# Row sums ahead of a subtraction, a copy moved to ScalarE, and three steps re-placed in a linear-attention and gated-MLP kernel

## The chip, the cores and the metric

The kernel runs on one core of a Trainium2 chip. The metric is the device time of one execution in microseconds (us). The core has five engines that run their own instruction lists in order and meet through semaphores: TensorE (PE in the profile; its weight loads are shown apart as PEld), VectorE (DVE), ScalarE (ACT), GpSimd (POOL) and SyncE (SP), which mostly issues DMAs.

## The reference

Two parts in a row. The first is an attention without a score matrix, for 8 batches, 8 heads, 576 rows and a head size of 64; the second an MLP with a gate on the 4608 rows of 512 that come out of it.

```python
q_s = exp(q - max(q, -1)); q_s = q_s / (sum(q_s, -1) + 1e-09)     # softmax along the head size
k_s = exp(k - max(k, 2));  k_s = k_s / (sum(k_s, 2) + 1e-09)      # softmax along the rows
kv  = einsum('bhsd,bhse->bhde', k_s, v)
x   = einsum('bhsd,bhde->bhse', q_s, kv)                          # then to [4608, 512]
h = x @ w_in                                                      # 512 -> 2048
g = h * (1.0 / (1.0 + exp(-beta * h)))
out = g @ w_out                                                   # 2048 -> 512
```

## The kernel before

**Slabs.** The rows are cut into nine slabs of 512. Slabs 0 to 7 hold the first 512 rows of each batch, slab 8 the 64 rows that each batch has left over. The main loop runs over `t`, the slab whose MLP is computed; the attention of a later batch (t + 1, and its preparation from t + 2 on) is woven into it.

**Pass 1** of a slab computes `h` transposed, 16 tiles of four matmuls of 128x512 (`pass1_tile`, with the first three tiles interleaved in `pass1_lead`). ScalarE evacuates each tile with Silu into GT (L746), VectorE scales it by 1/beta (`scale_g`, L769) and, after tiles 8, 12, 14 and 16, forms sums of halves of GT, GS1 and GS2 (L800, L805).

**Pass 2** of slab 0 is a plain product with WOUT (`pass2_group`). In the other slabs, `pass2_fast` forms the 2x2 block product with seven block products in place of eight, each of 16 matmuls of 128x256, in three PSUM banks: `s`, `z5` and `z2`. The order on TensorE is s and z5 interleaved, z2, then onto the same banks a second z5 product ("product 1" below), a second z2 product ("2"), a third z5 product ("3") and a third z2 product ("4"). Between them stand evacuations: TS gets a copy of s (L915), less z5 (L918), less z2 (L924); then ScalarE copies z5 and z2 to the output tile O2S (`copy`, L882), and VectorE adds TS to the last ones (`last`, L894). Since the later products add onto the same bank, product 1 may start only when L918 has read z5, product 2 when L924 has read z2, product 3 when the copy of z5 is done, and product 4 when the copy of z2 is done. `g_diff(0)` and `g_diff(1)` (L812, VectorE) turn halves of GT into differences that products 3 and 4 read.

**Attention of a batch.** ScalarE takes exps of q (EQ), k (EK) and the left-over k rows (EKR). `norm_main` has two parts: row sums and their reciprocals on VectorE (`sums`, L357 and L359, into QS and QI) and the multiplication EQ by QI (`mult`, L361, on GpSimd in the later slabs). `turn` has SP issue a DMA transpose of EQ into QT. `norm_turn` does all of this for two of four head pairs. `cast_v` (L377) and `cast_vr` (L391) cast v and its left-over rows to bf16 (VB, VR). `kv_steps` forms kv on TensorE (L482, for batches 0 and 1 L406), followed by VectorE's reciprocal RC (L490) and the scaled KVD (L449 or L459). `quad` and `out_step` multiply QT by KVD (L554, L406) into XT, the input of pass 1 of the next slab.

**Order of the work.** Each operation is recorded in the program's order with what it reads and writes; `Program.plan` derives from that the semaphore waits, and each engine gets its operations in the order recorded. Two devices place the side work. `todo` is a list of pairs (tick, function): each matmul of pass 1 is a tick (64 in all), each of pass 2 is 32/56 of one, and a function is recorded as soon as its tick is reached. `hooks` are lists of functions that `pass2_fast` records at its points `at(0)` (before s), `at(1)` (after the copy to TS), `at(2)` (after L918), `at(3)` (after L924), `at(4)` and `at(5)` (after ScalarE's copies of z5 and z2), `at(6)` and `at(7)` (after the two last additions). So in slabs 1 and 2 the eight exps stand on ScalarE behind the last Silu, the row sums on VectorE behind the subtractions L918 and L924, and `silu_table` loads ScalarE's table for the next pass 1 at `at(4)`.

**The end.** Each store has its own semaphore. Behind its last DMA, SP waits for all of them one after another (L149 to L151), in the order of their names.

Of the kernel before, what the change touches and what calls it, by code (L numbers as in the profile page):

```python
# [20 lines left out]
NG = NF // 2  # L21
# [8 lines left out]
PE, ACTE, DVE, POOL, SP = "tensor", "scalar", "vector", "gpsimd", "sync"  # L30
# [14 lines left out]
class Program:  # L45
# [12 lines left out]
    def add(self, eng, fn, r=(), w=(), bank=(), slot=None, after=(), war=False):  # L58
        op = Op(eng, fn, slot)
        op.pos = len(self.ops)  # L60
        deps = op.deps
        deps.extend(after)
        for k in r:
            deps.extend(self.writer.get(k, ()))
            self.readers.setdefault(k, []).append(op)
        for k in w:
            for d in self.readers.get(k, ()):
                if d is not op and (war or not self._same(d, op)):
                    deps.append(d)
            for d in self.writer.get(k, ()):  # L70
                if not self._same(d, op):
                    deps.append(d)
            self.readers[k] = []
            self.writer[k] = [op]
        for k in bank:
            t = self.touch.setdefault(k, {})
            for e, d in t.items():
                if e != eng:
                    deps.append(d)
            t[eng] = op  # L80
        if eng == POOL and slot is None:
            if self.pool is not None:
                deps.append(self.pool)
            self.pool = op
        self.ops.append(op)
        return op
# [42 lines left out]
    def emit(self, nc, es):  # L129
        counts, waits = self.plan()  # L130
        sems = {}
        for key in counts:
            sems[key] = es.enter_context(nc.semaphore("s_" + "_".join(str(x) for x in key)))
        by = {e: [] for e in (PE, ACTE, DVE, POOL, SP)}
        for op, w in zip(self.ops, waits):
            by[op.eng].append((op, w))

        def run(eng):
            def body(h):
                for op, w in by[eng]:  # L140
                    for key, n in w:
                        h.wait_ge(sems[key], n)
                    ins = op.fn(h)
                    if op.slot is not None:
                        ins.then_inc(sems[op.count[0]], 16)
                    elif op.inc:
                        ins.then_inc(sems[op.count[0]], 1)
                if eng == SP:
                    for key, n in sorted(counts.items(), key=str):  # L149
                        if key[0] == "dma" and str(key[1]).startswith("out"):  # L150
                            h.wait_ge(sems[key], n)  # L151
            return body

        with nc.Block() as blk:
            for e in (PE, ACTE, DVE, POOL, SP):
                getattr(blk, e)(run(e))


def bass_efficient_attn_shen__then__act_swish_beta_kernel(
# [12 lines left out]
    with ExitStack() as es:  # L172
        def sb(name, shape, dt):
# [33 lines left out]
        TS = sb("TS", [128, 512], F32)  # L207
# [12 lines left out]
        PS = [es.enter_context(nc.psum_tensor(f"PS{i}", [128, 512], F32)) for i in range(8)]  # L220
# [4 lines left out]
        P = Program()  # L225
        add = P.add
# [6 lines left out]
            r=["ts"], w=["idb"])  # L233
# [152 lines left out]
        def cast_vr(b, hs=(0, 1), after=()):  # L386
            pi = (b // 2) % 2
            for h in hs:
                o = bass.AP(VR[pi][h], 64 * h * NHP * VW, [[NHP * VW, 64], [HW, H], [1, D]])
                a = bass.AP(VRF, 64 * h * 512, [[512, 64], [D, H], [1, D]])  # L390
                add(POOL, lambda e, o=o, a=a: e.tensor_copy(o, a),  # L391
                    r=[("vrf", h), ("vrone", pi, h), ("vr0", pi, h)], w=[("vr", pi, h)],
                    after=after)
# [208 lines left out]
        def turn(b, hp0, n):  # L602
            i = b % 2
            o = bass.AP(QT[i], hp0 * 512, [[2048, 128], [128, 4 * n], [1, 128]])
            a = bass.AP(EQ[i], hp0 * 512, [[2048, 128], [1, 512 * n]])
            add(SP, lambda e: e.dma_start_transpose(o, a),
                r=[("eq", i, hp) for hp in range(hp0, hp0 + n)],
                w=[("qt", i, hp) for hp in range(hp0, hp0 + n)], slot=f"tq{i}{hp0}")
# [26 lines left out]

        def attn_late(b):
            if b < 4:
                x = 100 if b == 2 else 97
                return [(x, steps(kv_all, b)), (x + .1, lambda: g_diff(1)),
                        (118, one(quad, b, (0,)))]  # L640
            return [(96, steps(kv_all, b)), (99, lambda: g_diff(1)), (112, one(quad, b))]
# [193 lines left out]
        def pass2_fast(t, tick, hooks):  # L835
# [71 lines left out]
            def prod_s(part):  # L907
# [4 lines left out]
            prod(z5, *gs2(0), *wo(1, 1), True, False, range(0, 6))  # L912
            prod_s(range(6, NG))
            prod(z5, *gs2(0), *wo(1, 1), True, False, range(6, NG))
            add(DVE, lambda e: e.tensor_copy(TS[:, :], PS[s][:, :]), r=[("ps", s)], w=["ts"],  # L915
                bank=[s])
            at(1)
            add(DVE, lambda e: e.tensor_tensor(TS[:, :], TS[:, :], PS[z5][:, :], ALU.subtract),  # L918
                r=["ts", ("ps", z5)], w=["ts"], bank=[z5])
# [35 lines left out]
        for t in range(NSLAB):  # L955
            todo = []
            if t == 0:
                todo = [(x, steps(t_steps, 1, (hp,), NOW, ACTE))
                        for hp, x in enumerate((97, 106, 114, 119))]
                todo += [(107, one(exp_kr_s, 1))]  # L960
                todo += [(x, one(exp_k, 1, hp, 1)) for hp, x in enumerate((108, 115, 120, 125.5))]
                todo += [(x, one(cast_v, 1, hp, DVE))
                         for hp, x in ((1, 118.5), (2, 123), (3, 127))]
                todo += [(x, steps(kv_steps, 1, (hp,), NOW))
                         for hp, x in enumerate((118, 122, 126))]
                todo += [(x, steps(out_step, 1, hp, NOW, ACTE)) for hp, x in enumerate((122.5, 125))]
                todo += [(117, one(o2_evac, 0, 0, 3, ACTE))]
                todo += [(2, steps(out_step, 0, 3, HEAD, DVE))]
            elif t < 4:
                todo = attn_late(t + 1)  # L970
                if t > 1:
                    todo += [(1.5, one(quad, t, (1,)))]
                if t == 3:
                    todo += [(4, one(norm_turn, 4, 2))]
                if t == 1:
                    todo += [(1, steps(out_step, 1, 2, (3,), ACTE)),
                             (3, steps(kv_steps, 1, (3,), (7,))),
                             (6, steps(out_step, 1, 3, (7,), DVE)),
                             (6.1, one(w_sum, 2, 4, 4)), (6.2, one(w_diff, 0)),
                             (6.3, one(w_diff, 1))]  # L980
            elif t < 7:
                todo = attn(t + 1)
            elif t == 7:
                todo = spread(outr_steps(1), 32, 48)
# [59 lines left out]
            def on(n, fn, *a):  # L1044
                hooks.setdefault(n, []).append(lambda: fn(*a))
# [8 lines left out]
                add(ACTE, lambda e: e.activation(DUMMY[:, 2:3], WARM[:, 0:1], ACT.Silu),  # L1054
                    r=["warm"], w=["dummy"])

            def casts(b):
                g = P.writer[("gs2", NG - 1)]
                if b % 2 == 0:
                    cast_vr(b, after=g)  # L1060
                for hp in range(NHP):
                    cast_v(b, hp, after=g)

            if t == 1:
                on(0, exps, 2)
                on(0, casts, 2)
                on(2, norm_turn, 2, 0)
                on(3, norm_turn, 2, 2)
                on(3, g_diff, 0)
                on(4, silu_table)  # L1070
                on(3, load, 4)
            elif t == 2:
                on(0, exps, 3)
                on(2, norm_turn, 3, 0)
                on(3, norm_turn, 3, 2)
                on(3, g_diff, 0)
                on(3, load, 5)
                on(4, exp_q, 4)
                on(4, silu_table)
                on(4, casts, 4)  # L1080
                on(6, norm_turn, 4, 0)
            elif t == 3:
                on(0, exp_k, 4)
                on(0, exp_kr, 4)
                on(0, exp_q, 5)
                on(3, g_diff, 0)
                on(4, norm_turn, 5, 0)
                on(5, norm_turn, 5, 2)
                on(4, exp_qr, 1)
                on(5, exp_k, 5)  # L1090
                on(5, norm_turn_rem)
                on(5, casts, 5)
                on(5, load, 6)
                on(7, load_rem, "qrf", qt_h, QRF, 4)
            elif t + 2 < B:
                b = t + 2
                on(0, exps, b)
                on(0, casts, b)
                if t == 4:
                    on(0, load, 7)  # L1100
                on(3, norm_turn, b, 0)
                on(4, norm_turn, b, 2)
# [40 lines left out]
```

The softmax here doesn't subtract the row's maximum and nothing guards it: scores larger than these inputs give would overflow.

## Time and profile before

| | us |
|---|---|
| median of 5 runs | 273.04 |
| lowest, highest | 272.77, 274.46 |
| the profiled execution | 272.99 |
| its span, first to last instruction | 271.2 |
| TensorE's mean granted clock, share of full | 0.998 |
| slab 1, pass 1, from its first matmul | 45.7 to about 61 |
| slab 1, pass 2 | 60.9 to 75 |
| slab 2, pass 2 | 89.2 to 104 |
| last addition on VectorE (L894) | 267.61 to 268.03 |

A line of a timeline gives start, duration, engine, line, operation, output<-input with its shape, and in brackets how long the engine was idle before it and what released it. Rows that follow each other closely on an engine are merged (x2, x4). PEld rows show when TensorE was ready for a product: a wait of TensorE shows there first. "issue" as a releaser means that the profile shows nothing that was waited for.

### The profile page before, as it was taken

How to read it: one execution, taken by the hardware profiler on the slowest of the kernel's cores; microseconds unless marked ns; L12 is line 12 of the kernel's file. 1: busy time of each engine (PE TensorE's matmuls, PEld its weight loads, DVE VectorE, ACT ScalarE, POOL GpSimd, SP SyncE). 2: the span in 40 equal slices, each digit the busy share in tenths (PEclk: the TensorE clock that was granted, in tenths of full speed). 3: DMA queues.
4: the chain of work that ended last, by engine and by line, in shares of the span. 5: the costliest groups of instructions: out<-in, count | busy, mean ns of one | idle time of the engine just before them, and what ended most of it. 6: DMA issues, size and time to landing. Idle time of an engine off the chain costs nothing.

```text
span 271.2 us, 4991 instructions
## 1 busy us (share of the span) xinstructions
PE 263.0 (97%) x1974; PEld 163.5 (60%) x1993; DVE 193.2 (71%) x407; ACT 181.5 (67%) x289; POOL 63.5 (23%) x80
## 2 busy tenths in 40 slices
PE   8999999999999999999999999999999999999994
PEld 2544444348744875468645864587458745874683
DVE  4964586887957798868778876887588448626762
ACT  4898658799467974887778937892883387018610
POOL 2790000006630089100810680036000100000000
PEclk9999999999999999999999999999999999999999
DMA  7999999989699129940499899603600130012006
GB/s 219 318 204 206 228 324 350 297 232 372 161 324 324 51 47 290 288 155 2 77 268 273 245 360 178 195 3 78 213 2 0 36 140 2 0 64 93 0 1 156
DMA packets 59367, 45.95 MB, mean 169 GB/s; under 512 B 28608, under 2 KB 58320, under 8 KB 58320
## 3 DMA queue, kind: packets, MB, share of 16 engines
q1 hardware_dynamic: 54480, 40.90, 53.6%
q0 software_dynamic: 4240, 4.19, 9.4%
q10 hardware_dynamic: 624, 0.53, 0.6%
q8 instruction: 16, 0.26, 0.4%
q14 instruction: 7, 0.06, 0.1%
HBM read 36.71 MB, written 9.44 MB: 170 GB/s over the span
## 4 chain that ended last, share of the span: by engine, by line
PE 77%; DMA 9%; DVE 4%; POOL 4%; ACT 2%; issue 1%; SPq 0%; POOLq 0%
PE PS L406 43%; PE PS L846 31%; DMA WOUT<-in_moe_w_out_dram 5%; DMA QF<-in_q_dram 3%; POOL WIN L670 2%; PE PS L482 1%; PE PS L554 1%; DMA QT<-EQ 1%; DVE EQ L361 1%; DVE QS L357 1%; POOL EQ L361 1%; ACT EQ L319 1%; POOL VB L377 1%; ACT L1054 0%; POOL VR L391 0%
## 5 line engine op out<-in xcount | busy, mean ns | idle before, releaser
L406 PE MATMUL PS<-XT,WIN 128*128 128x512 bf16 x560 | 125.2, 379 | 1.2 <-issue 0.3
L746 ACT ACTIVATE GT<-PS,BETA 128x512 bf16<-128x512 f32 x144 | 95.2, 690 | 39.5 <-PE PS L406 39.2
L406 PEld LDWEIGHTS PS<-XT,WIN 128*128 128x128 bf16 x576 | 55.0, 98 | 64.8 <-DVE XT L596 0.7
L769 DVE TENSOR_SCALAR GT<-GT,RB 128x512 bf16<-128x512 bf16 x144 | 52.7, 387 | 38.4 <-ACT GT L746 37.6
L361 POOL TENSOR_TENSOR EQ<-EQ,QI 128x1024 bf16<-128x1024 bf16 (+1 forms) x13 | 25.6, 1968 | 47.2 <-DVE QI L359 46.5
L846 PE MATMUL PS<-WOUT,GS 128*128 128x256 bf16 x256 | 31.1, 273 | 0.0
L846 PE MATMUL PS<-WSUM,GT 128*128 128x256 bf16 x256 | 30.1, 273 | 1.0 <-ACT O2S L882 1.0
L846 PE MATMUL PS<-WOUT,GT 128*128 128x256 bf16 x256 | 29.8, 273 | 0.0
L846 PEld LDWEIGHTS PS<-WSUM,GT 128*128 128x128 bf16 x256 | 24.8, 98 | 5.0 <-ACT O2S L882 1.2
L882 ACT COPY O2S<-PS 128x512 f32<-128x512 f32 (+1 forms) x17 | 9.4, 560 | 26.1 <-PE PS L846 26.1
L846 PEld LDWEIGHTS PS<-WOUT,GT 128*128 128x128 bf16 x256 | 24.8, 98 | 2.9
L846 PEld LDWEIGHTS PS<-WOUT,GS 128*128 128x128 bf16 x256 | 24.8, 98 | 3.0
L319 ACT ACTIVATE EQ<-QF 128x512 bf16<-128x512 f32 x32 | 17.9, 620 | 7.3 <-DMA QF<-in_q_dram 7.3
L805 DVE TENSOR_TENSOR GS<-GT 128x512 bf16<-128x512 bf16 (+2 forms) x32 | 21.9, 685 | 0.0
L812 DVE TENSOR_TENSOR GT<-GT 128x2048 bf16<-128x2048 bf16 x16 | 21.7, 1381 | 0.0
L377 POOL CAST VB<-VF 128x512 bf16<-128x512 f32 x24 | 16.5, 688 | 22.0 <-DVE GS L805 13.3
L357 DVE TENSOR_REDUCE QS<-EQ 128x16 f32<-128x1024 bf16 (+1 forms) x20 | 19.7, 984 | 1.0 <-ACT EQ L319 1.0
L319 ACT ACTIVATE EK<-KF 128x512 bf16<-128x512 f32 x32 | 18.1, 620 | 0.0
L894 DVE TENSOR_TENSOR O2S<-TS,PS 128x512 f32<-128x512 f32 (+1 forms) x17 | 10.8, 647 | 9.6 <-PE PS L846 9.6
L846 PE MATMUL PS<-WSUM,GS 128*128 128x256 bf16 x128 | 16.6, 273 | 0.0
L406 PE MATMUL PS<-WOUT,GT 128*128 128x512 bf16 x62 | 15.0, 379 | 0.1
L846 PEld LDWEIGHTS PS<-WSUM,GS 128*128 128x128 bf16 x128 | 12.5, 98 | 3.2
(90 smaller groups left out, 208.9 us busy)
## 6 DMA issues: line engine op xcount, KB each, us to landing
out_dram<-O2S SPq DMA_DIRECT2D x8, 1024.0 KB, 4.9
QF<-in_q_dram SPq DMA_DIRECT2D x6, 1024.0 KB, 6.3
KF<-in_k_dram SPq DMA_DIRECT2D x6, 1024.0 KB, 9.5
VF<-in_v_dram SPq DMA_DIRECT2D x6, 1024.0 KB, 12.6
KF<-in_k_dram SPq DMA_DIRECT2D x8, 256.0 KB, 5.5
VF<-in_v_dram SPq DMA_DIRECT2D x8, 256.0 KB, 5.5
WOUT<-in_moe_w_out_dram POOLq DMA_DIRECT2D x4, 512.0 KB, 16.2
WIN<-in_moe_w_in_dram POOLq DMA_DIRECT2D x3, 512.0 KB, 9.0
```

The lines of the kernel that those rows point to most:

```text
L319: add(ACTE, lambda e, o=o, a=a: e.activation(o, a, ACT.Exp), r=[(name + "f", i, hp)], w=[("e" + name, i, hp)])
L357: add(DVE, lambda e: e.tensor_reduce(s_, a, AX.X, ALU.add), r=ks, w=[("qs", i, hp0)])
L361: add(eng, lambda e: e.tensor_tensor(a, a, vb, ALU.mult), r=ks + [("qi", i, hp0)], w=ks)
L377: add(eng, lambda e: (e.copy if eng == ACTE else e.tensor_copy)(o, a), r=[("vf", i, hp), ("vone", i)], w=[("vb", i, hp)], after=after)
L406: add(PE, lambda e: e.matmul(o, l, r_, start=start, stop=stop), r=r, w=w, bank=[bk])
L746: add(ACTE, lambda e: e.activation(GT[:, f, :], PS[bk][:, :], ACT.Silu, scale=BETA[:, f:f + 1]), r=[("ps", bk), "beta"], w=[("gt", f, 0), ...
L769: add(DVE, lambda e: e.tensor_scalar(GT[:, f, :], GT[:, f, :], RB[:, f:f + 1], None, ALU.mult), r=k + ["rb"], w=k)
L805: add(DVE, lambda e: e.tensor_tensor(GS2[:, i:i + n, :], GT[:, i:i + n, :], GT[:, i + NG:i + NG + n, :], ALU.add), r=[k_ for f in (i, i + ...
L812: add(DVE, lambda e: e.tensor_tensor(gv(f, th, NG), gv(f, th, NG), gv(f, 1 - th, NG), ALU.subtract), r=gk(f, 0, NG) + gk(f, 1, NG), w=gk(f ...
L846: add(PE, lambda e, l=l, r_=r_, st=st, u=u, i=i, b_=b_: e.matmul(PS[b_][:, 256 * u:256 * u + 256], l, r_, start=st, stop=end and i == NG - ...
L882: add(eng, lambda e, b_=b_, u0=u0, u1=u1: (e.copy if eng == ACTE else e.tensor_copy)(o[:, u0:u1, :], bank3(b_)[:, u0:u1, :]), r=[("ps", b_ ...
L894: add(DVE, lambda e, b_=b_, u0=u0, u1=u1: e.tensor_tensor(o[:, u0:u1, :], ts[:, u0:u1, :], bank3(b_)[:, u0:u1, :], ALU.add), r=["ts", ("ps ...
```

## The change

Six edits.

1. `Program.emit`: SP's final waits are put in the order in which the last store of each semaphore was recorded, in place of the order of their names.
2. `attn_late`: the kv steps of batch 2 (in slab 1) are recorded at tick 102 in place of 100, those of batch 3 (slab 2) at 98 in place of 97. g_diff(1), tied to them, moves along.
3. `pass2_fast`: the copy of s to TS is on ScalarE in slabs 1 and 2.
4. Slab 0: the cast of v for head pair 1 of batch 1 is recorded at tick 117.9 in place of 118.5, so ahead of the kv steps of head pair 0 (tick 118). On VectorE it now stands ahead of their RC and KVD.
5. Slabs 1 and 2: the exps are split. Two EQ exps stand at `at(0)`; the other two, the EK exps and EKR at `at(1)`, so that ScalarE's list is two exps, the copy to TS, six exps (and EKR in slab 1). The first row sums and reciprocals stand at `at(1)`, ahead of L918 on VectorE; the multiplication and the transpose stay at `at(2)`. In slab 1 the VR casts are released by the scaled tile `gt` 3 in place of the last GS2.
6. Slab 2: `silu_table` at `at(6)` in place of `at(4)`: on ScalarE it now follows the four exps of batch 4, the copy of z2 and the first XT copy.

```diff
+        last = {op.count[0]: op.pos for op in self.ops if op.slot is not None}
...
-                    for key, n in sorted(counts.items(), key=str):
-                        if key[0] == "dma" and str(key[1]).startswith("out"):
-                            h.wait_ge(sems[key], n)
+                    for key in sorted((k for k in counts if str(k[1]).startswith("out")),
+                                      key=lambda k: last[k]):
+                        h.wait_ge(sems[key], counts[key])
...
-                x = 100 if b == 2 else 97
+                x = 102 if b == 2 else 98
                 return [(x, steps(kv_all, b)), (x + .1, lambda: g_diff(1)),
                         (118, one(quad, b, (0,)))]
...
-            add(DVE, lambda e: e.tensor_copy(TS[:, :], PS[s][:, :]), r=[("ps", s)], w=["ts"],
-                bank=[s])
+            ce = ACTE if t < 3 else DVE
+            add(ce, lambda e: (e.copy if ce == ACTE else e.tensor_copy)(TS[:, :], PS[s][:, :]),
+                r=[("ps", s)], w=["ts"], bank=[s])
...
-                         for hp, x in ((1, 118.5), (2, 123), (3, 127))]
+                         for hp, x in ((1, 117.9), (2, 123), (3, 127))]
...
-            def casts(b):
+            def exps_split(b):
+                on(0, exp_q, b, 0, 2)
+                on(1, exp_q, b, 2, 2)
+                on(1, exp_k, b)
+                if b % 2 == 0:
+                    on(1, exp_kr, b)
+
+            def mult_turn(b, hp0):
+                norm_main(b, hp0, 2, POOL, sums=False)
+                turn(b, hp0, 2)
+
+            def casts(b, key=("gs2", NG - 1)):
                 g = P.writer[("gs2", NG - 1)]
                 if b % 2 == 0:
-                    cast_vr(b, after=g)
+                    cast_vr(b, after=P.writer[key])
...
             if t == 1:
-                on(0, exps, 2)
-                on(0, casts, 2)
-                on(2, norm_turn, 2, 0)
+                exps_split(2)
+                on(0, casts, 2, ("gt", 3, 0))
+                on(1, norm_main, 2, 0, 2, DVE, True, False)
+                on(2, mult_turn, 2, 0)
...
             elif t == 2:
-                on(0, exps, 3)
-                on(2, norm_turn, 3, 0)
+                exps_split(3)
+                on(1, norm_main, 3, 0, 2, DVE, True, False)
+                on(2, mult_turn, 3, 0)
...
-                on(4, silu_table)
+                on(6, silu_table)
```

## The prediction

> **What bounds the kernel now.** I read the page first, then the waits of the whole run, then the timeline around slab 0's end (36 to 51 us), slab 1's second pass (60 to 78) and slab 2's (90 to 106), one engine at a time.
>
> ```profile
> PE 263.0 (97%) x1974; PEld 163.5 (60%) x1993; DVE 193.2 (71%) x407; ACT 181.5 (67%) x289; POOL 63.5 (23%) x80
> PE 77%; DMA 9%; DVE 4%; POOL 4%; ACT 2%; issue 1%; SPq 0%; POOLq 0%
> ```
>
> TensorE works for 263.0 of 271.2 us at a granted clock of 0.998, and the change leaves its matmuls as they are. So only TensorE's gaps count. Three waits of the full list lie where the change works ("waited: us in total, times, longest"):
>
> ```profile
> PEld PS L554 <- DMA QT<-EQ: 1.3, 3, 0.6
> PEld PS L846 <- ACT O2S L882: 1.2, 1, 1.2
> PE PS L406 <- DVE VB L377: 0.4, 1, 0.4
> ```
>
> Their places, by engine (start, duration, idle before):
>
> ```profile
> 42.41 0.16 DVE L490 RECIPROCAL RC<-PS 128x1 f32<-128x1 f32 x1
> 42.60 0.35 DVE L449 SCALAR_TENSOR_TENSOR KVD<-PS,RC,MASK 128x128 bf16<-128x128 f32 x1
> 42.87 0.42 DVE L377 CAST VB<-VF 128x512 bf16<-128x512 f32 x1
> ...
> 64.18 0.69 DVE L915 COPY TS<-PS 128x512 f32<-128x512 f32 x1 [1.32 <-PE PS L846]
> 64.98 0.69 DVE L918 TENSOR_TENSOR TS<-TS,PS 128x512 f32<-128x512 f32 x1
> 65.58 1.21 DVE L357 TENSOR_REDUCE QS<-EQ 128x16 f32<-128x1024 bf16 x1
> 66.83 0.25 DVE L359 RECIPROCAL QI<-QS 128x16 f32<-128x16 f32 x1
> 67.00 0.63 DVE L924 TENSOR_TENSOR TS<-TS,PS 128x512 f32<-128x512 f32 x1
> ```
> ```profile
> 66.06 1.74 PEld L846 LDWEIGHTS PS<-WOUT,GT 128*128 128x128 bf16 x16
> ...
> 72.59 0.11 PEld L554 LDWEIGHTS PS<-QT,KVD 64*64 64x64 bf16 x4 [0.55 <-DMA QT<-EQ]
> ```
> ```profile
> 102.20 1.64 PEld L846 LDWEIGHTS PS<-WSUM,GT 128*128 128x128 bf16 x16 [1.16 <-ACT O2S L882]
> ```
> ```profile
> 100.18 1.28 ACT L1054 ACT_TABLE_LOAD   x1
> 101.47 0.20 ACT L1054 ACTIVATE DUMMY<-WARM 128x1 f32<-128x1 bf16 x1
> 101.58 0.57 ACT L882 COPY O2S<-PS 128x512 f32<-128x512 f32 x1
> ```
>
> See here that VectorE has no free moment from 64.18 on, that weight load 66.06 (product z5 again) follows the end of subtraction L918 (65.67) by only 0.39, and that slab 2's table load stands in front of the copy for which TensorE waits.
>
> **The change, part by part.** Times below are on the old profile's axis; a shift of TensorE carries on to the end, since it never catches up.
>
> *Slab 0, the cast moved ahead of RC and KVD.* The cast takes RC's place: 42.41 instead of 42.87, so 0.46 earlier. The matmul behind it starts 0.14 after the cast's end (43.29 to 43.43); it moves from 43.43 to 42.97, while TensorE's work ahead of it ended at 42.98. RC and KVD slide by the cast's pitch of 0.30 (40.90 to 41.20) and KVD ends at 43.25, where its reader, 43.72 before, is now due at 43.26: at most 0.1 lost there, and the next casts and KVDs hang on the same moved matmul. **-0.46**; bounds -0.5 and 0 (nothing, if another semaphore held it).
>
> *ScalarE's copy of TS.* Its own copies of this shape (L882) take 0.59 at a pitch of 0.48 (97.49 to 97.97); VectorE's took 0.69. The exps run at a pitch of 0.52 from 63.13, so the copy stands at 64.2, just when its product is ready (VectorE's copy began at 64.18), and everything behind it on ScalarE is 0.48 later. EKR, old end 67.91, ends at 68.39. Its matmul came at 68.12, so 0.3 would be lost in slab 1; the three matmuls (0.35) that the kv steps' new tick puts ahead of them, and the stall below, move it to 68.83. In slab 2 the last EK ends at 96.16 and is needed after 96.5. No cost. The kv steps' VectorE work (RC, KVD, g_diff(1)) keeps its place in that engine's list and starts behind g_diff(0), which ends later than the kv matmuls; it hides the later tick. The Trainium skill, ScalarE: Activation LUTs, section Rules for kernel authors, speaks against this: simple elementwise work belongs on VectorE, up to about three times faster in bf16. This copy is f32 out of PSUM, and the rows say 0.59 against 0.69 the other way round; by the rule's factor, three times 0.69, an estimate, the exps would be 2.1 late and the sum some 1 us worse in slab 1.
>
> *Row sums ahead of the subtraction.* The second exp ends at 63.13 + 0.52 + 0.62 = 64.27. The reduce starts at 64.30, the reciprocal 1.25 later, the z5 subtraction another 0.17 later at 65.72 (all pitches from the fence); it ends at 66.37, against 65.67. TensorE needs it at 66.06 and starts 0.05 after it (pattern of 76.63 to 76.68): 66.42. **A new stall of 0.36 in each of the two slabs.** Bounds 0.30 and 0.45. The z2 subtraction follows at 66.52 instead of 67.00, and the second row sums and g_diff(0) stand 0.42 earlier: g_diff(0) ends at 69.80, GpSimd's second product 1.75 after it (70.22 to 71.97 before), g_diff(1) 1.09 after that, at 72.64.
>
> *What it buys, slab 1.* QI is ready at 65.80 instead of 67.08. GpSimd must also be free: its four VB casts (2.65) ran from 64.48 since the two VR casts stood ahead at 63.00; those are now released by gt(3,0) and their own load (issued by 51.4, 5.6 to 7.2 to land), well before 61. VB ends at 65.65 and the product starts at 65.95, 1.28 earlier. The transpose, 3.39 to land, is there at 71.3. TensorE arrives at the first quad at 72.40 and loses only 0.22 to the change of tile shape (0.21 to 0.23 at the other "issue" rows) instead of 0.55. So slab 1 is +0.36 - 0.33 = **+0.03**.
>
> *Slab 2.* The stall moves product 4's start from 101.04 to 101.36 (QT's 0.05 comes off). ScalarE's copy of z2 now follows the four exps at once: z5's copy ends its wait at 97.86, exps from 98.34, copy 100.43 to 101.02: in time. Next in line is g_diff(1), by the same two steps (here 98.51 to 100.26 to 101.35 before): with g_diff(0) ending at 98.09 it ends at 100.93, in time too. So product 4 starts 0.84 earlier. But VectorE is then late: copy XT 101.36, O2S 101.96, reduce 102.56, reciprocal 103.79, last O2S 103.96 (TensorE was ready at 103.3), second XT 104.57 to 105.26, and TensorE, which waited for that XT until 105.70, goes on at 105.31. **-0.39**; bounds -0.84 and 0.
>
> *The silu table at hook 6* stands behind the first XT copy: 101.95 to 103.45 with its dummy; ScalarE's next XT is due at 104.1. Free; uncovered it would be 1.5. The Trainium skill, same page, section What ACT_TABLE_LOAD costs, adds a drain of 1.38 to the 1.28 of each switch. The rows show the dummy 1.29 after the load's start; with the drain that XT would end at some 105.4, an estimate, and cost 0.1.
>
> *SP's waits in order of issue.*
>
> ```profile
> L151 SPq EVENT_SEMAPHORE  x5: 28/28/1815, 268.7 to 270.7; - x5
> ```
>
> The long wait ends at 268.7 + 1.8 = 270.5; the other waits behind it end after 270.7. With the last store waited for last, they are over before: **-0.2**; bounds -0.25 and 0.
>
> *Sum:* -0.46 + 0.03 - 0.39 - 0.20 = **-1.02**. The profiled run took 272.99 (span 271.2 and 1.8 around it), 0.05 under the median of 273.04: 273.04 - 1.02 = 272.02.
>
> **Rivals.**
> A, *no new stall*: the subtraction comes in time after all, for instance because TensorE itself reaches 66.06 later. For: the margin is only 0.36 from chained pitches. Against: each pitch is a row, and VectorE takes its list in order. Then slab 1 gives -0.33 and slab 2's chain starts 0.36 sooner: -1.74, **271.3**.
> B, *the cast was not the wait* (part of the change does not do what it says). For: the weight load's idle of 0.91 before that matmul is put down to ScalarE's QT copy, which ends at 42.97. Against: that copy is of another bank, and the matmul's own wait names the cast. Without -0.46: **272.5**.
> C, *slower*: GpSimd's product, now at 65.95 instead of 67.23, holds up the z2 subtraction at 66.52 as it holds up g_diff(1) (2.12 instead of 1.26), until 67.86, 1.34 late. Then second row sums, g_diff(0), the second product and g_diff(1) are as late: 72.64 becomes 73.98, and product 4, due at 73.07, waits until 74.03: 0.96 in slab 1, as much in slab 2, sum -1.02 + 1.92 = +0.9: **273.9**. It decides from about 0.5 a slab. Against: at 67.00 that subtraction and at 67.54 a reduce ran beside the product at their plain 0.63 and 1.21.
>
> **How the numbers follow.** Forecast 0.58, A 0.20, B 0.15, C 0.07. Predicted 272.0. The range takes A and B in and the bounds of the single terms: 271.2 to 273.0; C is left out. About 0.5% (1.37 us) is what a measurement of this kernel tells from no change, so the borders are 271.67 and 274.41. Below the first: most of A and a fifth of the forecast, 0.29. Above the second: C only if dearer than worked out, 0.04. Within: 0.67.
>
> **What would show it.** Right: weight loads of L846 in slabs 1 and 2 that wait about 0.36 for DVE TS L918's line; no wait on QT in slab 1's first quad; no wait on O2S in slab 2, and a wait of 0.7 instead of 0.33 on the XT copy at slab 3's start; the VB wait at 43 us gone or under 0.1; no semaphore rows after SP's long wait. Wrong: no wait on TS (A), the kv matmul still at 43.4 (B), a z2 subtraction well over 0.7 us or far behind the z5 one (C).

## The result and the profile after

| | before | changed | ratio |
|---|---|---|---|
| median, us | 272.91 (51 runs) | 271.9 (27 runs) | 0.996 (0.9949 to 0.9971) |
| profiled execution, us | 272.99 | 271.65 | |
| its span, us | 271.2 | 269.7 | |

The kernel is 1.0 us faster by the medians, 272.0 were forecast. The two profiled executions are 1.3 apart (their spans 1.5); what lies between the two figures is treated below. In the experiments below one run, of 972.28 us in e1, is in the slow state and is left out of the figures.

The page of the changed kernel, busy time and chain by engine:

```profile
PE 262.5 (97%) x1974; PEld 163.3 (61%) x1993; DVE 191.6 (71%) x405; ACT 182.2 (68%) x291; POOL 63.7 (24%) x80
...
PE 89%; DVE 5%; DMA 2%; issue 1%; ACT 1%; POOL 1%; POOLq 0%
```

Its list of waits (total, times, longest, in us):

```profile
PEld PS L407 <- DVE XT L597: 1.1, 2, 0.7
...
PEld PS L847 <- DVE TS L920: 0.7, 2, 0.4
...
PEld PS L555 <- DMA QT<-EQ: 0.4, 1, 0.4
...
PE PS L407 <- DVE VB L378: 0.2, 1, 0.2
```

The wait on O2S is gone, that on QT fell from 1.3 to 0.4 and that on VB from 0.4 to 0.2. New is one on TS, in two places, and the wait on XT grew. The timelines show where. VectorE of the changed kernel, slab 0 and slab 1:

```profile
42.13 0.42 DVE L378 CAST VB<-VF 128x512 bf16<-128x512 f32 x1
42.47 0.16 DVE L491 RECIPROCAL RC<-PS 128x1 f32<-128x1 f32 x1
...
63.58 1.22 DVE L358 TENSOR_REDUCE QS<-EQ 128x16 f32<-128x1024 bf16 x1 [1.45 <-ACT EQ L320]
64.83 0.25 DVE L360 RECIPROCAL QI<-QS 128x16 f32<-128x16 f32 x1
65.00 0.63 DVE L920 TENSOR_TENSOR TS<-TS,PS 128x512 f32<-128x512 f32 x1
65.74 0.69 DVE L926 TENSOR_TENSOR TS<-TS,PS 128x512 f32<-128x512 f32 x1
```

TensorE's weight loads of the changed kernel, slabs 1 and 2:

```profile
65.69 1.97 PEld L847 LDWEIGHTS PS<-WOUT,GT 128*128 128x128 bf16 x19 [0.37 <-DVE TS L920]
...
71.99 0.11 PEld L555 LDWEIGHTS PS<-QT,KVD 64*64 64x64 bf16 x4 [0.42 <-DMA QT<-EQ]
...
100.40 1.75 PEld L847 LDWEIGHTS PS<-WSUM,GT 128*128 128x128 bf16 x17 [0.23 <-issue]
...
104.42 3.57 PEld L407 LDWEIGHTS PS<-XT,WIN 128*128 128x128 bf16 x18 [0.75 <-DVE XT L597]
```

ScalarE of the changed kernel, slab 2:

```profile
97.64 2.19 ACT L320 ACTIVATE EQ<-QF 128x512 bf16<-128x512 f32 x4
99.73 0.57 ACT L883 COPY O2S<-PS 128x512 f32<-128x512 f32 x1
100.60 0.59 ACT L597 CAST XT<-PS 128x512 bf16<-128x512 f32 x1 [0.30 <-PE PS L555]
101.20 1.28 ACT L1056 ACT_TABLE_LOAD   x1
```

Read them together: the z5 subtraction (L920) now ends at 65.63 and TensorE's next product waits 0.37 for it. The copy O2S follows the exps and ends at 100.30, before product 4's first weights, so the wait of 1.16 is gone (seventeen loads in one row, where before the sixteen of product 4 stood apart behind their wait). Part of this is handed back at 104.42, in the wait for XT.

To see which stage gave what, take three weight loads that can be found in each profile: the one behind the XT wait early in slab 1's first pass (before: 49.04), in slab 2's (76.68) and in slab 3's (105.70). Their differences are the stages; "end" is the span less the last.

| kernel | to slab 1 | slab 1 | slab 2 | slab 3 to the end |
|---|---|---|---|---|
| before | 49.04 | 27.64 | 29.02 | 165.5 |
| changed | 48.31 | 27.63 | 28.48 | 165.3 |
| difference | -0.73 | -0.01 | -0.54 | -0.2 |

The forecast's terms were -0.46, +0.03, -0.39 and -0.2.

### The profile page after: what moved, and what is told of

It reads as the page before. It is cut to its first block, busy times and chain, and to the rows that moved or that the text cites. A ratio compares the mean times of both kernels' runs of the same rounds, so it can differ in the third digit from the quotient of the medians.

```text
span 269.7 us, 4993 instructions
## 1 busy us (share of the span) xinstructions
PE 262.5 (97%) x1974; PEld 163.3 (61%) x1993; DVE 191.6 (71%) x405; ACT 182.2 (68%) x291; POOL 63.7 (24%) x80
## 3 DMA queue, kind: packets, MB, share of 16 engines
q1 hardware_dynamic: 54480, 40.90, 53.7%
## 4 chain that ended last, share of the span: by engine, by line
PE 89%; DVE 5%; DMA 2%; issue 1%; ACT 1%; POOL 1%; POOLq 0%
PE PS L407 54%; PE PS L847 32%; DMA QT<-EQ 2%; DVE QS L358 2%; PE PS L555 1%; PE PS L483 1%; POOL EQ L362 1%; PE PS L405 1%; DVE O2S L895 1%; DVE EQ L362 1%; DVE QI L360 1%; DVE XT L597 0%; ACT L320 0%; ACT EQ L320 0%; DVE XT L512 0%
```

## The experiments

Each is timed against the kernel before on the same chip; 95% intervals in brackets. The runs stand on four chips, so that a difference of two medians is rough. The stages are those of the table above, each from one profiled execution.

| run | median, us | ratio | to slab 1 | slab 1 | slab 2 | end |
|---|---|---|---|---|---|---|
| e1 | 272.66 | 1.0002 (0.999 to 1.0015) | 48.71 | 27.65 | 29.01 | 165.5 |
| e12 | 272.66 | 0.9992 (0.9983 to 1.0001) | 48.64 | 27.64 | 29.02 | 165.5 |
| e2 | 272.64 | 0.9998 (0.9989 to 1.0007) | 48.38 | 27.64 | 29.02 | 165.3 |
| e3 | 272.29 | 0.9982 (0.9974 to 0.9991) | 48.77 | 27.65 | 28.47 | 165.6 |
| e4 | 273.21 | 1.0021 (1.0008 to 1.0034) | 48.70 | 27.47 | 29.43 | 165.5 |
| e9 | 272.16 | 0.9982 (0.997 to 0.9995) | 48.69 | 27.42 | 28.48 | 165.3 |
| e10 | 271.74 | 0.9962 (0.9943 to 0.9982) | 48.24 | 27.64 | 28.46 | 165.4 |
| e8 | 271.92 | 0.9974 (0.9954 to 0.9993) | 48.29 | 27.63 | 28.48 | 165.3 |
| e5 | 271.37 | 0.9957 (0.9945 to 0.9969) | 48.20 | 27.47 | 28.29 | 165.3 |
| e6 | 271.63 | 0.9963 (0.995 to 0.9977) | 48.38 | 27.73 | 28.06 | 165.3 |
| e7 | 271.67 | 0.9965 (0.9954 to 0.9977) | 48.34 | 27.87 | 28.11 | 165.3 |
| e11 | 271.05 | 0.9942 (0.9926 to 0.9957) | 48.27 | 27.47 | 28.11 | 165.2 |

**The moved cast alone: e1, again as e12, and taken back out of the changed kernel: e9.**

```diff
-                         for hp, x in ((1, 118.5), (2, 123), (3, 127))]
+                         for hp, x in ((1, 117.9), (2, 123), (3, 127))]
```

> The kernel before with the cast of head pair 1 moved to tick 117.9 alone. Forecast's theory (the kv matmul of head pair 1 hung on this cast): TensorE's row at that place has no wait on VB over 0.2, and the time falls by 0.4 to 0.5 us, ratio 0.998 to 0.9985. Rival B (something else held that matmul): no change, ratio 1.000. In the profile the cast starts right behind the WSUM row. A second cause is looked for: if GpSimd's VRS cast and VectorE's third EQ product near 39 us meet, the EQ product takes 1.15 instead of 0.69 and everything up to slab 1 is 0.27 later, in any kernel.

> The changed kernel with the cast of head pair 1 back at tick 118.5. In all profiles so far the kv matmuls of head pairs 0 and 1 start 1.53 to 1.54 apart with the moved cast and 1.71 to 2.00 apart without; so the cast should be worth 0.2 to 0.46: from 1.54 back to 1.7 to 2.0 in the profile, and 0.2 to 0.45 us slower than the changed kernel, ratio to before 0.997 to 0.998. Rival (the time of the cast alone, ratio 1.0002, is right and nothing is gained): same time as the changed kernel, 0.996.

> The kernel before with the moved cast alone, a second time, since its first time (ratio 1.0002, 0.999 to 1.0015) speaks against the 0.46 that its profile shows between the kv matmuls of head pairs 0 and 1. If the cast is worth what the profiles show and the first time was drawn from late arrivals of slab 0's loads: ratio 0.998 to 0.999, kv 0 to kv 1 again 1.54, and the start of slab 1's second pass at 60.1 to 60.3 unless GpSimd's VRS cast holds up the third EQ product (1.1 instead of 0.69), then 60.6. Rival (worth nothing alone): ratio 1.000 again with an undisturbed slab 0.

The distance between the weight loads for the kv matmuls of head pairs 0 and 1 is 2.00, 1.71, 2.00, 1.94 and 2.00 in the five profiles without the moved cast (before, e2, e3, e4, e9), and 1.37 in e10 and 1.53 to 1.54 in the other eight with it. The matmul itself starts 0.14 to 0.15 after the end of the cast in all profiles but e10, with and without the edit. So it did hang on the cast. Weight loads of e9 and of e12:

```profile
41.05 0.24 PEld L407 LDWEIGHTS PS<-VB,EK 128*128 128x128 bf16 x4 [0.39 <-ACT QT L425]
...
43.05 0.24 PEld L407 LDWEIGHTS PS<-VB,EK 128*128 128x128 bf16 x4 [0.91 <-ACT QT L425]
```
```profile
41.46 0.24 PEld L406 LDWEIGHTS PS<-VB,EK 128*128 128x128 bf16 x4 [0.38 <-ACT QT L424]
...
43.00 0.24 PEld L406 LDWEIGHTS PS<-VB,EK 128*128 128x128 bf16 x4 [0.45 <-ACT O2S L773]
```

The second row is 2.00 behind the first in e9 and 1.54 in e12. But the first moves by itself, from 41.03 to 41.54 over all profiles. It follows VectorE's work, and that follows the loads of slab 0. In e12 the third EQ exp waited for its load until 37.54; in the changed kernel until 37.14. In the profile of before the loads were in time, but GpSimd's VRS cast met VectorE's EQ product. GpSimd and VectorE, before:

```profile
38.99 0.61 POOL L383 CAST VRS<-VRF 128x512 bf16<-128x512 f32 x1 [18.50 <-DMA VRF<-in_v_dram]
```
```profile
39.01 1.15 DVE L361 TENSOR_TENSOR EQ<-EQ,QI 128x512 bf16<-128x512 bf16 x1
```

and in the changed kernel:

```profile
39.11 0.98 POOL L384 CAST VRS<-VRF 128x512 bf16<-128x512 f32 x1 [18.63 <-DMA VRF<-in_v_dram]
```
```profile
38.93 0.69 DVE L362 TENSOR_TENSOR EQ<-EQ,QI 128x512 bf16<-128x512 bf16 x1
```

Whichever of the two starts first runs at its plain length and the other is drawn out: 0.61 and 1.15 one way, 0.98 and 0.69 the other. Of the 0.73 by which the first stages of the two profiled executions differ, this is 0.27: e3, which has neither the moved cast nor a drawn-out EQ product, reaches slab 1 at 48.77, between 49.04 and 48.31. It comes with an execution, not with the change.

In time the cast alone gives 1.0002 and 0.9992, which leaves anything from nothing to 0.46 (the first interval alone ends at 0.27). Taken out of the changed kernel it costs 0.26 by the medians and 0.6 by the ratios, 0.38 in the stage to slab 1, of which slab 1 gives 0.21 back, since QT there landed at 71.65, before TensorE came for it. The profiles show on what the worth depends. Without the edit the second kv matmul comes 2.53 to 2.59 behind the start of VectorE's first VB cast; with it 2.07 to 2.11, and 2.33 in e10, where TensorE is busy until the matmul starts at 42.62. That first cast starts at 40.18 in e2 and at 40.51 to 40.90 in the four others without the edit. So in e2 VectorE was early, and the kv matmul came at 42.77 without the edit, only 0.15 behind that of e10 (first cast at 40.30). Where VectorE is late, the edit is worth the difference of the two distances, some 0.46. How much of 0.46 an average execution keeps stays open.

**The order of SP's final waits alone: e2.** The diff is that of `Program.emit`.

> The kernel before with SP's final waits in order of the stores alone. Forecast's theory: 0.2 us off the end, ratio about 0.9992, seen as SP's semaphore rows that end with the last landing; rival: nothing, since the last landing and not the rows sets the end. Up to the last matmul nothing may differ.

SP's rows in the changed kernel:

```profile
L152 SPq EVENT_SEMAPHORE  x6: 17/28/28, 267.9 to 269.3; - x6
```

No long wait is followed by short ones any more. The last stage is 165.3 in e2 as in the changed kernel (165.2 to 165.4 in every kernel with this order), 165.5 to 165.6 without. The ratio, 0.9998 (0.9989 to 1.0007), can't tell 0.2 us from nothing.

**The table load alone: e3.**

```diff
-                on(4, silu_table)
+                on(6, silu_table)
```

> The kernel before with the silu table at hook 6 in slab 2 alone. Theory (the table load in front of the z2 copy was the whole wait in slab 2): the copy ends at about 100.75 instead of 102.15, product 4 then waits for g_diff(1), which ends at 101.35, and starts about 0.8 earlier; VectorE's chain of O2S, row sums, O2S and XT gives part of it back, so slab 3's first pass starts 0.45 to 0.55 earlier, ratio about 0.998. Rival (the split of the exps and the early row sums are needed for it): under 0.2 us.

Slab 2 falls from 29.02 to 28.47, as in the whole change, and the time by 0.49 by the ratio (0.9982). e3's weight loads in slab 2:

```profile
101.20 1.66 PEld L846 LDWEIGHTS PS<-WSUM,GT 128*128 128x128 bf16 x16 [0.41 <-issue]
...
104.89 2.06 PEld L406 LDWEIGHTS PS<-XT,WIN 128*128 128x128 bf16 x11 [0.51 <-DVE XT L596]
```

Product 4 waits 0.41 in place of 1.16; with the copy O2S ending at 100.37 it is g_diff(1), ending at 101.09, that comes last, as expected. The theory holds.

**The split, the copy on ScalarE and the early row sums: alone (e4), and left out of the change (e10).** e4 is the changed kernel without the diffs of e1, e2 and e3; e10 is the kernel before with these three.

> The changed kernel without the moved cast, the moved table load and the order of the final waits: so the split exps, ScalarE's copy of TS, the early row sums, the released VR casts and the later kv ticks alone. Forecast's theory: stalls of TensorE on the z5 subtraction in slabs 1 and 2 of 0.28 to 0.37 each; slab 1 even; in slab 2 the table load is still in front of the z2 copy and the stall only makes it later, so +0.2 to +0.4 us, ratio 1.0007 to 1.0015. Rival A (no stall, the early transposes pay): -0.3 to -0.6 us.

> The kernel before with the moved cast, the moved table load and the order of the final waits, so the change without the split exps, the copy on ScalarE, the early row sums, the released VR casts and the later kv ticks. Theory (these are worth nothing beside the three others): time of the changed kernel, ratio 0.9955 to 0.9965; from the start of slab 1's second pass to slab 2's 28.3 us, on to slab 3's 28.46. Rival (they carry part of the gain): ratio 0.9975 or more.

e4 is slower, 1.0021, by 0.54 where 0.2 to 0.4 were expected; slab 2 is 0.41 longer, since the wait on O2S is still there and the stall makes it later:

```profile
94.19 1.21 PEld L846 LDWEIGHTS PS<-WOUT,GT 128*128 128x128 bf16 x12 [0.37 <-DVE TS L919]
...
102.09 1.64 PEld L846 LDWEIGHTS PS<-WSUM,GT 128*128 128x128 bf16 x16 [1.38 <-ACT O2S L882]
```

(The span of e4's profile, 271.1, is no longer than that of before, because its first stage, where it has no edit, came out 0.34 shorter.) e10 has the span of the changed kernel, 269.7, its stages within 0.1 and its ratio, though the interval of that ratio alone would leave room for the rival. By the stages, beside the other three edits this part of the change is worth nothing: it puts a stall on TS (0.37) in place of the waits in front of product 4 (0.39 and 0.43 in e10's slabs 1 and 2).

**What sets QT in slab 1: e8.**

```diff
-                on(0, casts, 2, ("gt", 3, 0))
+                on(0, casts, 2)
```

> The changed kernel with the VR casts released by the last GS2 again. GpSimd's first product in slab 1 starts about 1.1 later and the transpose is issued at about 68.3 instead of 67.2. Theory now (the bulk loads, which end at about 68, set the landing and not the issue): QT lands within 0.3 of the changed kernel's 71.95, time within 0.2 us of it. The forecast's theory (3.4 from issue to landing whatever runs beside it): no difference either from 71.3 to 71.7, and a wait of 0.2 only. Rival (4.8 from any issue): QT at 73.1, 1.1 us slower.

Transposes on SP, changed kernel and e8. Each row holds two transposes, and its length is SP's, not that of the landing; the line below it has the time from issue to landing:

```profile
67.16 4.78 SPq L607 DMA_TRANSPOSE QT<-EQ  x2
...
DMA to landing us min/median/max: 3.1/4.0/4.8
```
```profile
68.39 4.07 SPq L607 DMA_TRANSPOSE QT<-EQ  x2
...
DMA to landing us min/median/max: 3.3/3.4/3.5
```

And the quad's weight loads in e8:

```profile
71.90 0.11 PEld L555 LDWEIGHTS PS<-QT,KVD 64*64 64x64 bf16 x4 [0.35 <-DMA QT<-EQ]
```

Issued 1.23 later, QT is used 0.09 earlier, 71.90 instead of 71.99. The landing took 4.8 from the early issue and 3.5 from the late one. So it isn't the issue that sets the landing here: a fixed 3.4 fails in the changed kernel, a fixed 4.8 in e8.

What does set it can be read from the landing of slab 0's store, which SP issued before the transposes. Store and time to its landing, before and changed:

```profile
58.59 3.22 SPq L779 DMA_DIRECT2D out_dram<-O2S  x1
...
out_dram<-O2S SPq DMA_DIRECT2D x1, 1024.0 KB, 13.1
```
```profile
58.97 2.85 SPq L780 DMA_DIRECT2D out_dram<-O2S  x1
...
out_dram<-O2S SPq DMA_DIRECT2D x1, 1024.0 KB, 12.1
```

| kernel | store landed | first transpose issued | it landed | behind its issue | behind the store |
|---|---|---|---|---|---|
| before | 71.69 | 69.16 | 72.55 | 3.39 | 0.9 |
| changed | 71.04 | 67.16 | 71.95 | 4.78 | 0.9 |
| e8 | 71.00 | 68.39 | 71.86 | 3.47 | 0.9 |
| e7 | 71.33 | 68.28 | 72.21 | 3.93 | 0.9 |
| e10 | 70.23 | 68.36 | 71.50 | 3.15 | 1.3 |

In ten of the thirteen profiles with the store in this place the transpose landed 0.85 to 0.92 behind the store, whatever its issue. In the other three (e1, e2, e10), where the store landed by 70.5, it landed 3.14 or 3.15 behind its own issue.

**VectorE's order put right: e5 (first row sums behind the z5 subtraction), e6 (batch 4's first row sums behind slab 3's second quad), e7 (both), e11 (both, and slab 0's store behind the transposes).**

```diff
-                on(1, norm_main, 2, 0, 2, DVE, True, False)
-                on(2, mult_turn, 2, 0)
+                on(2, norm_turn, 2, 0)
...
-                on(6, norm_turn, 4, 0)
...
-                    todo += [(4, one(norm_turn, 4, 2))]
+                    todo += [(4, one(norm_turn, 4, 0)), (4.1, one(norm_turn, 4, 2))]
...
-                    if n == 10:
-                        store(0)
...
+                on(3, store, 0)
```

The first three lines stand for slab 1 and the like for slab 2 (e5, e7, e11), the next for e6, e7 and e11, the last for e11.

> The changed kernel with the first row sums back behind the z5 subtraction (ScalarE keeps the copy of TS). Theory (the order of VectorE made the stall): no wait of TensorE on that subtraction in either slab, 0.28 gained in each; QT is issued about 1.0 later in slab 1 but lands no later than about 72.0, since in the changed kernel it took 4.8 instead of 3.4 to land behind the bulk loads; so 0.2 to 0.5 us faster than the changed kernel, about 271.5, ratio to before 0.9945 to 0.995. Rival (the early row sums are worth their stall): slower than the changed kernel by 0.3 to 0.7, QT waits of 0.7 to 1.3.

> The changed kernel with batch 4's first row sums recorded behind slab 3's second quad, so not between the last two additions and the XT copy on VectorE. Theory (this chain gave back part of slab 2's gain): the wait on XT at slab 3's start falls from 0.75 to 0.33 and the time by 0.4 us, about 271.5, ratio 0.9945 to 0.995. Rival (the row sums are only shifted and delay the GT scaling or batch 4's transposes): no gain, or a new wait of TensorE in slab 3.

> Both: the first row sums behind the z5 subtraction and batch 4's behind slab 3's second quad. If both theories hold the gains add: 0.6 to 0.9 us faster than the changed kernel, about 271.1, ratio 0.993 to 0.9938.

> The kernel with both sets of row sums later, and slab 0's store issued behind slab 1's two transposes instead of before slab 1's second pass. Theory (QT's landing in slab 1 is set by the bulk transfers, 4 MB from 55.8 on, of which the store is 1): the bulk ends some 2 to 3 us earlier, QT lands 3.1 to 3.4 after its issue, at about 71.5, and TensorE's wait on it in slab 1 falls from 0.41 to 0.91 to under 0.3; time 0.2 to 0.6 under the same kernel with the early store, about 271.1. Rival (the transposes' landing hangs on something else): wait unchanged, time unchanged.

e5 has no wait on TS and gains 0.19 in slab 2 and 0.16 in slab 1, where 0.28 each were expected. In slab 2 product 4 then waits 0.31 for g_diff(1), and the gain lies in the XT wait, 0.51 instead of 0.75. e6 gains 0.42 in slab 2; its XT wait is back at the 0.33 of other slabs:

```profile
104.17 2.92 PEld L407 LDWEIGHTS PS<-XT,WIN 128*128 128x128 bf16 x15 [0.33 <-DVE XT L597]
```

The gains did not add: e7, expected at 271.1, came to 271.67. Its slab 2 is 0.37 under the changed kernel's, no better than e6's: with the XT wait at 0.33 already, the stall on TS only gives way to the 0.31 at product 4. And QT arrived late in slab 1. By the ratios e5, e6 and e7 (0.9957, 0.9963, 0.9965) can't be told from the changed kernel (0.996); their gains are those of single profiles. e11 takes the store out of the way. Quad of slab 1 in e7 and in e11:

```profile
72.25 0.11 PEld L555 LDWEIGHTS PS<-QT,KVD 64*64 64x64 bf16 x4 [0.91 <-DMA QT<-EQ]
```
```profile
71.48 0.11 PEld L555 LDWEIGHTS PS<-QT,KVD 64*64 64x64 bf16 x4 [0.21 <-DMA QT<-EQ]
```

From 0.91 to 0.21, as at the other changes of tile shape; QT landed 3.1 to 3.2 after its issue, as expected with the store gone from in front of it. With 271.05 and a ratio of 0.9942 (0.9926 to 0.9957), e11 is the fastest kernel measured here, 0.85 under the changed one by the medians and 0.5 by the ratios; it has six runs, and the two intervals overlap a little.

## Why the prediction was right, and where its terms were off

**What bounds it.** Right: only TensorE's gaps moved. From slab 3's first pass to the last matmul nothing changed.

**The sum, -1.02.** The medians gave -1.01, and this closeness is in part luck. Slab 1, slab 2 and the end measured some -0.7 together where -0.56 were forecast. So about 0.3 are left for slab 0 in an average execution (an estimate, 1.0 less 0.7), not 0.46: two misses of much the same size cancel.

**Slab 0, -0.46.** The mechanism was right: 2.00 became 1.54 between the two kv weight loads. Rival B falls on the profiles. The size that reaches the time is not settled (e1, e12, e9): the profiles give 0.15 where VectorE is early and 0.46 where it is late. The 0.73 of the two profiled executions holds 0.27 of another cause, the meeting on GpSimd and VectorE, and so makes the result look larger than it is.

**The new stall, 0.36.** The wait was there in every profile with this order, 0.37 each time, so rival A falls. But it costs TensorE less, 0.26: from the first matmul of pass 2 to the first of product 3 it took 9.6 in both slabs before (60.92 to 70.52, 89.22 to 98.81) and 9.85 to 9.86 in the changed kernel (60.20 to 70.05, 88.47 to 98.33). A weight load normally stands 0.11 ahead of its matmul (66.06 and 66.17 before); behind the wait both start at 65.69, so that this lead is used up and comes off the 0.37. The worked-out end of the subtraction, 66.37, does not come out of the rows named (65.72 makes 66.41 with a row of 0.69 and 66.35 with one of 0.63); the error is small beside the bounds.

**Slab 1, +0.03.** Measured -0.01, but by other parts than worked out: QT did not land 3.39 after its issue but 4.78, so its wait fell only from 0.55 to 0.42 instead of to 0.22. What paid for that was the smaller stall and 0.14 at product 4, which had waited on g_diff(1) (17 loads in 1.89 before, 1.75 after): +0.26 - 0.13 - 0.14 = -0.01. The step that failed is "the transpose, 3.39 to land". It took a duration from one row as if it belonged to the transpose; in that row too the landing came 0.9 behind slab 0's store. In the changed kernel the issue came 2.00 earlier (0.73 of it from slab 0) and the landing only 0.60, like that of the store (0.65). So the early row sums did not bring the QT that they were to bring.

**Slab 2, -0.39.** Measured -0.54. The order of the waits was as forecast, down to the XT wait (0.7 forecast, 0.75 measured); the difference is the smaller stall, which brought VectorE's chain 0.08 forward, and a pitch of 0.54 instead of 0.61 between the last O2S and the XT copy (103.15 to 103.69). e3 shows that the table load alone gives all of it.

**The copy on ScalarE and the silu table.** Free, as forecast, by the profile (no run moves the copy alone): 0.58 for the copy in slab 1, and EKR was in time. The load and its dummy ended at 102.70, the next XT came at 103.33. The drain that the Trainium skill (ScalarE: Activation LUTs, What ACT_TABLE_LOAD costs) adds does not show, as the dummy starts 1.30 after the load, at 102.50. The same page's advice to keep simple elementwise work on VectorE (Rules for kernel authors), whose factor is one for bf16, does not carry over to this copy in f32: 0.58 on ScalarE, 0.69 on VectorE.

**Rival C** falls too: with GpSimd's product from 65.24 on, the z2 subtraction ran from 65.74 in its plain 0.69.

**SP, -0.2.** The profiles agree; the time alone can't show it.

## What to carry to other kernels

Where an operation is put ahead of another on an in-order engine, compare the slack of the one it overtakes with its own length before counting what it releases: here the row sums took 1.4 us in front of a subtraction with 0.39 to spare, and the gain went into the stall. Do not carry a DMA's time from issue to landing from one place to another: here the transpose landed 0.9 behind a store issued before it, and taking that store away shortened the time where issuing the transpose 1.23 earlier brought nothing forward. When two edits shorten the same chain, look which wait comes next before adding their gains: in slab 2 the stall on TS stood in front of another wait of much the same length. And when a change moves some tenths of a per cent, cut the profiles into stages at the same instructions: slab 2 and all behind it repeated to 0.1 us in kernels that left them alone, while the loads at the start moved the first stage by 0.4 and more and the whole time by more than the effect.

## What the runs showed of the hardware

Two operations of GpSimd and VectorE that meet can run one after the other: 0.61 and 1.15 or 0.98 and 0.69, by which came first, with a start 0.02 to 0.18 apart; the z2 subtraction and the row sums beside GpSimd's product kept their 0.69 and 1.21. In all profiles the second then ended 0.47 to 0.55 after the first. The same transpose took from 3.1 to 4.9 to land (e6 the longest): 0.85 to 0.92 behind slab 0's store in ten profiles, 3.14 to 3.16 behind its own issue in the three where the store landed early and in e11, where it is issued later. That the store and not the loads beside it decides rests on these profiles and on that one run.
